# Queries turned raw in float32 and split behind the turn; tokens routed in four batches of blocks

## The chip, the cores and the metric

The kernel runs on one core of one Trainium2 chip. The metric is the device time of one execution in microseconds; of the kernel before, three runs gave 1262.17, 1265.66 and 1268.53 us, median 1265.66. One execution was profiled; it took 1265.35 us.

The engines are TensorE (PE in the profile, its weight loads PEld), VectorE (DVE), ScalarE (ACT), GpSimd (POOL) and SyncE (SP, which here only issues loads and stores). Each works off its own list of instructions in a fixed order.

## The reference, cut to what matters

Three layers follow each other: attention over the 32 largest scores of each query, a gated feed-forward layer on the normalized result, and a layer of 8 experts of which each token uses one.

```python
scores = scale * np.matmul(q, k.transpose(0, 1, 3, 2))        # 4 batches, 8 heads, 576 queries, 64 wide
kth = np.partition(scores, -32, axis=-1)[..., -32:-31]
scores = np.where(scores >= kth, scores, -1000000000.0)
attn = np.exp(scores - max); attn = attn / (attn.sum + 1e-9)
x = (attn @ v)                                                 # to 2304 tokens x 512
xn = x / sqrt(mean(x * x) + 1e-6) * rms_g
x = (silu(xn @ w_gate) * (xn @ w_val)) @ w_out                 # 512 -> 1536 -> 512
logits = x @ gate2 + modality_bias[modality_id]                # 8 experts
e_idx = argmax(logits); gate_w = softmax(logits)[e_idx]
out[mask_e] = gate_w * (relu(x[mask_e] @ w1[e]) @ w2[e])       # 512 -> 1024 -> 512
```

## The kernel before, in words

The kernel has a front, which computes attention, the feed-forward layer and the routing of the tokens, and a second part, which goes over the 8 experts.

**Attention.** The queries are cut into tiles of 128, and a step has two tiles; there are 72 steps (`steps`). For each tile TensorE makes the scores (`qk`, L526), ScalarE copies them to SBUF (L539), VectorE finds the 32nd largest score by rounds of MAX8 and MATCH_REPLACE8 (`topk`, L561 and L564, fed by L541 to L543), ScalarE and GpSimd mask and exponentiate (`soft0` to `soft3`), TensorE turns the result (`tr`, L621) and multiplies it by the values (`av`, L667). The scores need more precision than one pass of TensorE has, so every query is held as two float32r numbers: its rounded part and the rest.

**How a query is split before.** `dma_q` loads the two tiles of a step, 64 columns each. `split_q` makes the two parts on GpSimd: L452 rounds by adding zero, with each query written twice side by side, so that it lies in both halves of the 128 partitions after the turn; L453 subtracts the rounded part from the query. `trans_q` turns the four blocks (two tiles, two parts) on TensorE (L461), and one copy of 512 columns on ScalarE takes them out of PSUM into `qS` (L469, or L474 for the leftover queries). The load stands six steps ahead of the use, the split four, the turn two.

**Feed-forward layer.** As soon as all heads of a block of 128 tokens are done, the block, or a pair of blocks, is a granule; there are 17 granules with 18 blocks. A granule is a list of small pieces (`norm`, `xtr`, `ff1`, `ff2`), which `step` takes from a queue between the pieces of attention. The matrix products are in pairs of float16 parts, three products each (`mm3`, L746). The weights come in float32; VectorE picks their bits apart (`convert_weights`, L275, L280, L284), ScalarE makes the rounded part (L290, L292), GpSimd the rest (L293); the 12 pieces of `w_out` come first, the 24 of the other two later, while attention runs already. `gate_columns` folds the routing matrix into `w_out`, so `ff2` gives 8 more columns, the logits.

**Routing before.** Behind each granule, `ff2` adds the bias (L805) and calls `route`: 12 small VectorE instructions (L838 to L854) and one exponential on ScalarE find the expert, the one-hot `O` and the gate weight of each token of the granule. `rank`, a piece that goes into the queue of the next granule behind its first two products, counts on TensorE how many earlier tokens went to the same expert: for each block one product of a full matrix of ones with the sum so far `acc_oh` (L865), one of a triangle of ones with the block's own `O` (L866), and for the second block of a pair one with the first's `O` (L864). Its result stands in a bank of `ps_f`, of which there are two, shared with `ff1` and `ff2`. VectorE then adds (L875, L878, L879), makes slots (L880), advances `acc_oh` (L882), fills the payload (L884, L885), and GpSimd writes token number and weight into the expert's table by an indirect DMA per block (L887).

**What sets the order.** The program is written in the order of `step`, with high priority nowhere. The framework's scheduler then reorders each engine's list by a model of the times, so an edit at one place can move instructions far from it.

## Time and profile before

| | |
|---|---|
| runs | 1262.17, 1265.66, 1268.53 us |
| profiled execution | 1265.35 us, of which the span of instructions is 1263.7 us |
| busy, of the span | PE 90%, PEld 83%, DVE 73%, ACT 66%, POOL 58% |
| attention | ends near 828 us |
| feed-forward layer | first product at 171 us, last near 927 us |
| experts | from 946 us to the end |
| granted clock of TensorE | 0.929 of full speed over the span |

A busy time counts an engine as busy from the start of an instruction to its end. On TensorE and VectorE one instruction starts before the one ahead of it has ended, so busy times overlap; what an instruction costs its engine in a dense stretch is read from the start of one to the start of the next. In the tables of waits a line names the engine, tile and line that waited, then the engine, tile and line that released it, then the total in us, how many times, and the longest. The granted clock is given as a share of 2.4 GHz; 0.50 is the lower of its two levels, 1.2 GHz, and a value between is a mean over the stretch. In a row of the timeline "x4" means four instructions in a row, and the second number is from the start of the first to the end of the last.

### The profile page before, as it was taken

To read this page: it belongs to the slowest core of one execution; us is meant where nothing else is said; L and a number is where in the kernel's file an instruction comes from. 1 tells how busy PE (TensorE), PEld (TensorE's weight loads), DVE (VectorE), ACT (ScalarE), POOL (GpSimd) and SP (SyncE) were. 2 spreads that over 40 slices of the span, in tenths; PEclk is the share of its full clock that TensorE was granted. 3 is DMA by queue.
4 is the path that set the end of the run, shared out by engine and by line. 5 is a ranking of instruction groups with operands and counts; after the bars stand their busy time and mean duration, and the time that the engine had idled before them with its cause. 6 is when DMAs were issued, how large, how long until landed. Compare 5 with 4: busy or idle time off the path is not lost. (4 is left out here: it accounts for less than half of the span.)

```text
span 1263.7 us, 32277 instructions
## 1 busy us (share of the span) xinstructions
PE 1140.6 (90%) x12286; PEld 1044.3 (83%) x12286; DVE 927.7 (73%) x2883; ACT 833.3 (66%) x1757; POOL 738.8 (58%) x850
## 2 busy tenths in 40 slices
PE   6976777989999999999999999999948898999985
PEld 6965667988999999999898999999937897798884
DVE  7999999669999999999999999921115434254251
ACT  5868888677888888888998788753315434354251
POOL 7866767668857888777798767643423222022120
PEclk9856677989999999999999999999978998999998
DMA  8143312011000111000011000000029525354130
GB/s 289 51 126 84 96 44 79 14 45 48 9 17 17 28 40 53 17 8 18 23 38 40 17 15 10 2 11 19 2 71 348 185 73 209 109 184 139 70 116 18
DMA packets 68894, 87.80 MB, mean 69 GB/s; under 512 B 34386, under 2 KB 43734, under 8 KB 68696
## 3 DMA queue, kind: packets, MB, share of 16 engines
q1 hardware_dynamic: 60152, 63.66, 16.3%
q0 software_dynamic: 6320, 16.31, 3.8%
q10 hardware_dynamic: 2224, 5.25, 1.2%
q8 instruction: 117, 1.92, 0.7%
q14 instruction: 81, 0.66, 0.2%
HBM read 75.58 MB, written 10.92 MB: 68 GB/s over the span
## 5 line engine op out<-in xcount | busy, mean ns | idle before, releaser
L561 DVE MAX8 w<-w 128x8 f32<-128x296 f32 x576 | 249.8, 456 | 1.2
L595 POOL TENSOR_TENSOR s<-s,r 128x576 f32<-128x576 f32 x144 | 201.2, 1419 | 31.8 <-ACT r L591 31.5
L564 DVE MATCH_REPLACE8 w<-w 128x296 f32<-128x296 f32 x432 | 193.1, 449 | 0.0
L746 PE MATMUL pf<-xT,wg 128*128 128x128 f16 (+1 forms) x2448 | 172.5, 224 | 5.0 <-DVE T L875 2.9
L746 PE MATMUL pf<-xT,wv 128*128 128x128 f16 (+1 forms) x2448 | 168.8, 223 | 0.3 <-ACT xf L735 0.3
L746 PEld LDWEIGHTS <-wg 128*128 128x128 f16 x2448 | 148.8, 99 | 11.4 <-issue 5.4
L746 PE MATMUL po<-wo,h 128*128 128x264 f16 (+1 forms) x1296 | 157.4, 275 | 0.9 <-ACT t L773 0.9
L526 PE MATMUL ps<-kS,qS 128*128 128x288 f32 x640 | 138.4, 345 | 21.2 <-DVE w L542 20.3
L746 PEld LDWEIGHTS <-wv 128*128 128x128 f16 x2448 | 146.5, 98 | 4.6 <-issue 0.4
L746 PEld LDWEIGHTS <-h 128*128 128x128 f16 x1296 | 121.9, 98 | 18.8 <-issue 1.4
L1236 POOL DMA_INDIRECT out_dram<-o,idx x23 | 22.8, 993 | 195.7 <-ACT o L1235 139.6
L1180 DVE SCALAR_TENSOR_TENSOR hl<-ph,hh 128x256 fp32r<-128x256 f32 x88 | 36.9, 421 | 132.0 <-ACT hh L1179 129.0
L526 PEld LDWEIGHTS ps<-kS,qS 128*128 128x128 f32 x640 | 103.9, 215 | 24.4 <-ACT r L591 14.8
L599 ACT ACTIVATE s<-s,mbs 128x576 f32<-128x576 f32 x144 | 113.3, 788 | 13.5 <-POOL s L595 13.1
L1177 PE MATMUL ph<-xh,wh 128*128 128x256 f32 x352 | 101.5, 291 | 16.4 <-PEq L1294 16.0
L591 ACT ACTIVATE r<-s,mbs 128x576 f32<-128x576 f32 x144 | 104.9, 779 | 13.9 <-POOL mbs L582 13.8
L621 PE MATMUL pt<-identr,s 128*128 128x128 f32 x576 | 98.2, 302 | 14.8 <-ACT s L599 13.7
L539 ACT COPY s<-ps 128x576 f32<-128x576 f32 x144 | 93.2, 647 | 21.8 <-PE ps L526 21.2
L1177 PE MATMUL ph<-xl,wh 128*128 128x256 f32 x352 | 100.3, 286 | 0.0
L1177 PE MATMUL ph<-xh,wl 128*128 128x256 f32 x352 | 100.3, 286 | 0.0
L778 POOL TENSOR_TENSOR t<-u,t 128x512 f32<-128x512 f32 x54 | 69.6, 1290 | 48.1 <-ACT t L773 28.8
L667 PE MATMUL pt<-vs,pT 128*128 128x64 f16 (+1 forms) x1680 | 88.4, 198 | 8.7 <-POOL pT L635 6.0
(204 smaller groups left out, 2825.1 us busy)
## 6 DMA issues: line engine op xcount, KB each, us to landing
wr<-in_moe_w_dram SPq DMA_DIRECT2D x48, 512.0 KB
wst<-in_moe_w_gate_dram SPq DMA_DIRECT2D x24, 256.0 KB
wst<-in_moe_w_val_dram SPq DMA_DIRECT2D x24, 256.0 KB
wr<-in_moe_w_dram ACTq DMA_DIRECT2D x10, 512.0 KB
kr<-in_k_dram SPq DMA_DIRECT2D x32, 128.0 KB
vt<-in_v_dram SPq DMA_DIRECT2D x32, 128.0 KB
x_d<-xo SPq DMA_DIRECT2D x16, 256.0 KB
qr<-in_q_dram SPq DMA_DIRECT2D x112, 32.0 KB
```

Of the source, the lines that this page charges most:

```text
L526: nc.tensor.matmul(out=ps[:, a, 0:HS], lhsT=qS[i // 2][:, i % 2, j, o2:o2 + 128], rhs=kt[:, m, ks], start=(n == 0), stop=(n == len(ops) - 1),)
L539: nc.scalar.copy(out=s.rearrange("p (a k) -> p a k", a=2), in_=ps[:, :, 0:HS])
L561: steps.append(lambda: dve.max(lists[t][:, 8 * r:8 * r + 8], src[t] if r == 0 else dst[t]))
L564: steps.append(lambda: dve.match_replace(out=dst[t], in_to_replace=lists[t][:, 8 * r:8 * r + 8], in_values=src[t] if r == 0 else dst[t], i ...
L591: nc.scalar.activation(out=d["r"], in_=d["s"], func=AF.Relu, scale=-BIG, bias=d["mb"][:, 1:2])
L595: nc.gpsimd.tensor_tensor(out=d["s"], in0=d["s"], in1=d.pop("r"), op=OP.subtract)
L599: nc.scalar.activation(out=d["s"], in_=d["s"], func=AF.Exp, scale=SCALE, bias=d["mb"][:, 0:1], accum_out=d["rs"])
L621: nc.tensor.transpose(pt[:, c * 128:(c + 1) * 128], e[:, e0 + c * 128:e0 + (c + 1) * 128], ident)
L667: nc.tensor.matmul(out=av_[o:o + n], lhsT=l, rhs=r, start=(a == 0), stop=(a == len(ops) - 1))
L746: nc.tensor.matmul(out=out_, lhsT=l, rhs=r, start=(a == 0), stop=(a == len(ops) - 1))
L778: nc.gpsimd.tensor_tensor(out=t, in0=u, in1=t, op=OP.mult)
L1177: nc.tensor.matmul(out=pt, lhsT=l[:, fs], rhs=r[:, kk, :], start=(n == 0), stop=(n == 3 * KD - 1))
```

## The change

**Queries.** `dma_q` loads each query twice, into both halves of a tile of 128 columns, and does so four steps ahead instead of six. `split_q` is gone. `trans_q` turns the raw float32 queries, two blocks instead of four. Behind that ScalarE copies the 256 columns out of PSUM twice, once rounded to float32r straight into `qS` and once as they are into `qf`, and GpSimd subtracts one from the other into the second part of `qS`.

**Routing.** The granules are put into four batches that end with the granules 5, 10, 15 and 16: 6, 6, 5 and 1 blocks. `ff2` writes its logits into the batch's tile, and `route` and `rank` run once for a batch, behind its last granule, over all its blocks. In `rank` a block has one product with each earlier block of its batch. An assertion on the number of steps goes; nothing else changes.

```diff
+    NG = len(granules)
+    ENDS = [NG // 3, 2 * NG // 3 - 1, NG - 2, NG - 1]
+    batches = [
+        [blk for g in range(lo + 1, hi + 1) for blk in granules[g][1]] for lo, hi in zip([-1] + ENDS[:-1], ENDS)
+    ]
+    NBM = max(len(bl) for bl in batches)
...
         def dma_q(s):
-            qr = ap_.tile([128, 2, D], F32, name="qr", tag="qr", bufs=QB)
+            qr = ap_.tile([128, 2, 2, D], F32, name="qr", tag="qr", bufs=QB)
...
+            for j in range(2):
+                if hh is not None and t1[2] == hh:
+                    src = q[b, 2 * p + hh, 0:SM, :].rearrange("(p c) d -> p c d", c=CM)
+                    nc.sync.dma_start(out=qr[:, :, j, :], in_=src[:, c:c + 2, :])
+                    continue
...
-        def split_q(s):
-            qr = raw.pop(("q", s))
-            qs = ap_.tile([128, 2, 2, 2, D], F32R, name="qs", tag="qs", bufs=2)
-            z = zero.unsqueeze(2).unsqueeze(3).to_broadcast([128, 2, 2, D])
-            q2 = qr.unsqueeze(2).to_broadcast([128, 2, 2, D])
-            nc.gpsimd.tensor_tensor(out=qs[:, :, 0], in0=q2, in1=z, op=OP.add)
-            nc.gpsimd.tensor_tensor(out=qs[:, :, 1], in0=q2, in1=qs[:, :, 0].bitcast(F32), op=OP.subtract)
-            raw["qs", s] = qs
...
         def trans_q(s):
-            qs = raw.pop(("qs", s))
-            pt = ps_m.tile([128, 512], F32R, name="pq", tag="sm")
+            qr = raw.pop(("q", s))
+            pt = ps_m.tile([128, 512], F32, name="pq", tag="sm")
             for t in range(2):
-                for j in range(2):
-                    nc.tensor.transpose(
-                        pt[:, (2 * t + j) * 128:(2 * t + j + 1) * 128],
-                        qs[:, t, j].rearrange("p a d -> p (a d)"),
-                        identr,
-                    )
+                nc.tensor.transpose(
+                    pt[:, t * 128:(t + 1) * 128], qr[:, t].rearrange("p a d -> p (a d)"), ident
+                )
...
+            def post():
+                qf = ap_.tile([128, 2, 128], F32, name="qf", tag="qf", bufs=2)
+                nc.scalar.copy(out=hi, in_=cut(src))
+                nc.scalar.copy(out=qf, in_=src)
+                nc.gpsimd.tensor_tensor(out=lo, in0=cut(qf), in1=hi.bitcast(F32), op=OP.subtract)
...
-                at(s - 6, lambda s=s: dma_q(s))
+                at(s - 4, lambda s=s: dma_q(s))
...
-            at(s - 4, lambda s=s: split_q(s))
...
-                        if j == 0:
-                            rt["L"] = mp.tile([128, 2, E], F32, name="L", tag="L", bufs=1)[:, 0:nb]
+                        if bi not in logits:
+                            logits[bi] = mp.tile([128, NBM, E], F32, name="L", tag="L", bufs=1)
...
-                        if j == nb - 1:
+                        if j == nb - 1 and gi in ENDS:
                             route()
...
-                    for j in range(nb):
+                    for j in range(nr):
                         o = pt[:, j * E:(j + 1) * E]
                         for j2 in range(j):
                             nc.tensor.matmul(out=o, lhsT=ones16, rhs=O[:, j2, :], start=(j2 == 0), stop=False)
...
-            return pre, hid, res, [rank()]
+            return pre, hid, res, [rank()] if gi in ENDS else []
```

The instructions of `route` and of the second half of `rank` stay as they are, over `nr` blocks of the batch instead of `nb` of the granule.

The scheduler also orders the first tens of microseconds anew. On SP the loads of the program's start stand like this before (`qr` is the query tile, `kr` the keys; `wg`, `wv` with L262 are the pieces of `w_out`, which are loaded into the room of the other weights):

```order
L262 DMA wg_105<-in_moe_w_out_dram 128x1024 x2
L371 DMA kr<-in_k_dram 128x256
L374 DMA kr<-in_k_dram 64x64
L371 DMA kr<-in_k_dram 128x256
L374 DMA kr<-in_k_dram 64x64
L441 DMA qr<-in_q_dram 128x64 x2
L262 DMA wg_105<-in_moe_w_out_dram 128x1024
```

and after the change, from the load that follows the first keys on:

```order
L268 DMA wg_105<-in_moe_w_out_dram 128x1024
L268 DMA wg_106<-in_moe_w_out_dram 128x1024 x3
L151 DMA gate_sb<-in_moe_w_gate_dram 128x4x8
L152 DMA g_sb<-in_moe_rms_g_dram 128x4x1
L268 DMA wv_107<-in_moe_w_out_dram 128x1024 x3
L268 DMA wv_108<-in_moe_w_out_dram 128x1024
L377 DMA kr<-in_k_dram 128x256
L380 DMA kr<-in_k_dram 64x64
L377 DMA kr<-in_k_dram 128x256
L380 DMA kr<-in_k_dram 64x64
L268 DMA wv_108<-in_moe_w_out_dram 128x1024 x2
L450 DMA qr<-in_q_dram 128x64 x12
```

The first queries were the seventh load; now 22 loads stand ahead of them, all 12 pieces of `w_out` among these.

On GpSimd the first split of a query stood second in the work on the start's data (`ks` are the split keys, `wo` the rests of `w_out`, `qs` the split queries):

```order
L405 TENSOR_TENSOR ks<-kr,zero 128x9x64
L452 TENSOR_TENSOR qs<-qr,zero 128x2x128
L406 TENSOR_TENSOR ks<-kr,ks 128x9x64
L293 TENSOR_TENSOR wo_110<-wf,wo_109 128x2x256
L453 TENSOR_TENSOR qs<-qr,qs 128x2x128
```

and now the first difference that makes a query complete (L479) stands behind nine of the twelve rests:

```order
L412 TENSOR_TENSOR ks<-kr,ks 128x9x64
L299 TENSOR_TENSOR wo_110<-wf,wo_109 128x2x256 x3
L153 TENSOR_SCALAR gs_sb<-g_sb 128x4
L299 TENSOR_TENSOR wo_110<-wf,wo_109 128x2x256 x3
L411 TENSOR_TENSOR ks<-kr,zero 128x9x64
L299 TENSOR_TENSOR wo_110<-wf,wo_109 128x2x256
L412 TENSOR_TENSOR ks<-kr,ks 128x9x64
L208 MEMSET room 128x288
L299 TENSOR_TENSOR wo_110<-wf,wo_109 128x2x256
L209 IOTA room 128x144
L299 TENSOR_TENSOR wo_110<-wf,wo_109 128x2x256
L479 TENSOR_TENSOR qS<-qf,qS 128x2x128
```

On VectorE the first scores (`w<-s,ps`, then MAX) came behind 20 of the 36 instructions that pick apart `w_out` (`wp`):

```order
L275 TENSOR_SCALAR wp<-wv_107 128x512
L284 SCALAR_TENSOR_TENSOR wp<-wg_106,wp 128x512
L280 SCALAR_TENSOR_TENSOR wp<-wv_107,wp 128x512
L541 TENSOR_TENSOR w<-s,ps 128x288
L542 TENSOR_TENSOR w<-s,ps 128x288
L284 SCALAR_TENSOR_TENSOR wp<-wv_107,wp 128x512
L543 MAX w<-w 128x8
```

and now come behind all 36:

```order
L281 TENSOR_SCALAR wp<-wv_108 128x512
L286 SCALAR_TENSOR_TENSOR wp<-wv_108,wp 128x512
L290 SCALAR_TENSOR_TENSOR wp<-wv_108,wp 128x512
L547 TENSOR_TENSOR w<-s,ps 128x288
L548 TENSOR_TENSOR w<-s,ps 128x288
L549 MAX w<-w 128x8
```

From there on the two sorts of work, which were mixed, follow each other.

## Rows read from the trace of the kernel before

**Rows 1.** Windows; columns: stretch, length, busy (count) of PE, PEld, DVE, ACT, POOL; PEclk

```profile
60.00:220.00 160.00, 116.08 (x776) 101.75 (x775) 160.00 (x534) 130.26 (x277) 113.78 (x132) 0.66 0.30 86
220.00:340.00 120.00, 114.04 (x1483) 104.57 (x1483) 96.42 (x324) 92.29 (x205) 87.66 (x103) 0.95 0.11 30
340.00:820.00 480.00, 476.60 (x6392) 440.82 (x6392) 465.16 (x1581) 400.03 (x894) 367.43 (x425) 1.00 0.08 23
820.00:928.00 108.00, 105.85 (x1572) 100.37 (x1569) 25.37 (x132) 40.60 (x87) 44.45 (x46) 1.00 0.04 12
928.00:1263.00 335.00, 281.87 (x1771) 252.00 (x1770) 130.17 (x191) 128.35 (x211) 77.25 (x77) 0.92 0.42 143
```

**Rows 2.** Waits of PE between 340 and 820 us, the longest

```profile
PE pf L746 <- DVE u L768: 1.2, 1, 1.2
```

**Rows 3.** Timeline of PE at 507 us

```profile
507.27 0.94 PE L746 MATMUL pf<-xT,wv 128*128 128x128 f16 x14
508.05 0.61 PE L621 MATMUL pt<-identr,s 128*128 128x128 f32 x4
508.49 0.27 PE L626 MATMUL sm<-identr,s 128*128 128x128 f32 x1
508.52 0.54 PE L461 MATMUL pq<-identr,qs 128*128 128x128 f32 x4
508.90 1.18 PE L746 MATMUL pf<-xT,wv 128*128 128x128 f16 x18
```

**Rows 4.** Timeline of DVE at 525 us

```profile
525.19 0.14 DVE L838 TENSOR_REDUCE mx<-L 128x1 f32<-128x8 f32 x1
525.25 0.15 DVE L843 TENSOR_TENSOR d<-L 128x8 f32<-128x8 f32 x1
525.32 0.46 DVE L561 MAX8 w<-w 128x8 f32<-128x296 f32 x1
```

**Rows 5.** Line L878 on DVE: duration in ns, least, median, most

```profile
L878 DVE TENSOR_TENSOR T<-T,O x17: 154/346/1335, 276.0 to 926.6; 128x8 f32<-128x8 f32 x16, 128x16 f32<-128x16 f32 x1
```

**Rows 6.** Line L875 on DVE: who waited for it, us and times

```profile
  PE pf L746: 2.9, 6
  PE ps L526: 0.8, 1
```

**Rows 7.** Timeline of PE at a rank, 857 us

```profile
857.07 0.17 PE L866 MATMUL pr<-O,tri 128*128 128x8 f16 x1
857.57 2.84 PE L746 MATMUL pf<-xT,wg 128*128 128x128 f16 x48 [0.33 <-DVE T L875]
```

**Rows 8.** Turns of queries: L461 at 220 to 340 us, its group at 340 to 820 us

```profile
L461 PE MATMUL pq<-identr,qs x40: 225/249/366, 220.5 to 335.9; 128*128 128x128 f32 x40
...
L461 PE MATMUL pq<-identr,qs 128*128 128x128 f32 x172 | 24.0, 255 | 0.0
```

**Rows 9.** Timeline of SP and DVE in the first 20 us

```profile
17.78 4.10 SPq L441 DMA_DIRECT2D qr<-in_q_dram  x6
...
18.93 0.69 DVE L280 SCALAR_TENSOR_TENSOR wp<-wv,wp 128x512 int32<-128x512 int32 x1
19.53 0.45 DVE L541 TENSOR_TENSOR w<-s,ps 128x288 f32<-128x288 f32 x1
```

**Rows 10.** Waits of DVE between 0 and 60 us, the longest

```profile
DVE wp L275 <- DMA wg<-in_moe_w_out_dram: 4.3, 2, 2.6
```

**Rows 11.** Groups on POOL, 340 to 820 us: count, busy, mean ns, idle before

```profile
L595 POOL TENSOR_TENSOR s<-s,r 128x576 f32<-128x576 f32 x92 | 128.7, 1421 | 20.7 <-ACT r L591 20.4
...
L453 POOL TENSOR_TENSOR qs<-qr,qs 128x256 fp32r<-128x256 f32 x41 | 30.1, 734 | 1.4
...
L452 POOL TENSOR_TENSOR qs<-qr,zero 128x256 fp32r<-128x256 f32 x41 | 25.5, 621 | 22.0 <-PE pq L461 21.8
```

**Rows 12.** Timeline of POOL in the last granule

```profile
906.45 1.01 POOL L887 DMA_INDIRECT tab_d<-pay,si  x1 [0.15 <-issue]
910.90 1.28 POOL L778 TENSOR_TENSOR t<-u,t 128x512 f32<-128x512 f32 x1 [2.25 <-ACT t L773]
```

More of the change, by code (lines that the diff above doesn't have):

```diff
@@ L131, in topk_attention_swiglu_moe_kernel @@
     margin = const.tile([128, 1], F32, name="margin")
-    finite = const.tile([128, len(granules)], F32, name="finite")
+    finite = const.tile([128, len(batches)], F32, name="finite")
     sumsq = const.tile([128, 4], F32, name="sumsq")
@@ L472, in trans_q @@
[L472 to L474 removed]
+                hi, lo, cut = dst[:, :, 0], dst[:, :, 1], lambda x: x
+            else:
+                dst = qS[s] = ap_.tile([128, 2, 2, 192], F32R, name="qS", tag="qS", bufs=2)
+                nc.gpsimd.memset(dst[:, :, :, 64:128].bitcast(F32), 0.0)
+                heads = dst.rearrange("p t j (i r) -> p t j i r", i=3)
+                hi, lo = heads[:, :, 0, 0::2], heads[:, :, 1, 0::2]
+                cut = lambda x: x.rearrange("p t (i r) -> p t i r", i=2)
@@ L689, in granule @@
             G = 512 // n
+            bi, batch = next((i, bl) for i, bl in enumerate(batches) if blocks[0] in bl)
             x = [xn.pop(j) for j in blocks]
@@ L880, in post @@
                     last_ = nc.vector.tensor_copy(si, sl)
-                    for j in range(nb):
+                    for j in range(nr):
                         nc.vector.tensor_tensor(out=acc_oh, in0=acc_oh, in1=O[:, j, :], op=OP.add)
                     with tc.issue_after(last_.ins):
-                        nc.vector.tensor_copy(pay[:, :, 0], tok[:, blocks[0]:blocks[0] + nb])
+                        j = 0
+                        while j < nr:
+                            n2 = 1
+                            while j + n2 < nr and batch[j + n2] == batch[j] + n2:
+                                n2 += 1
+                            nc.vector.tensor_copy(pay[:, j:j + n2, 0], tok[:, batch[j]:batch[j] + n2])
+                            j += n2
                         nc.vector.tensor_copy(pay[:, :, 1].bitcast(F32), rt["gt"])
-                    for j in range(nb):
+                    for j in range(nr):
                         nc.gpsimd.indirect_dma_start(
```

56 lines of the change are left out of this document (25 added, 31 removed).

## The prediction

> **What bounds the kernel now.** I read the busy times by stage first [rows 1]. Five stretches show five different states. From 60 to 220 us DVE is busy for all of 160 us, while PE stands idle for 44 of them at a granted clock of 0.66: scores and the picking apart of weights share VectorE, and it sets the pace. From 340 to 820 us PE is busy for 476.6 of 480 us at full clock and DVE for 465.2, so both look full and the table alone doesn't decide. From 820 to 928 us PE works off what is left of the feed-forward layer, DVE being nearly idle. From 928 us on the experts run, which the change doesn't touch: 335 us on both sides.
>
> Which of the two bounds the long stretch is read from the waits and from start-to-start times. PE's longest wait of the whole 480 us is 1.2 us [rows 2]. Busy times of PE overlap, so I check in the timeline that it is really dense [rows 3]: 14 float16 products of 128 columns take 0.78 us from the first start to the next group, 56 ns each, where 128 columns at 2.4 GHz need 53; the groups follow without a gap. PE is full there in earnest. DVE is less full than it looks: a routing instruction is counted with 0.14 us, but the next one starts 0.06 to 0.07 us later [rows 4]. So from 220 to 928 us I count every piece of work by what it takes from PE, and before 220 us by what it takes from DVE.
>
> **Turning the queries.** Four float32r turns of a step hold PE for 508.90 - 508.52 = 0.38 us; four float32 turns of another tile take 508.49 - 508.05 = 0.44 us, so the two new ones take 0.22 [rows 3]. A step saves 0.16 us. Of the turns 40 lie between 220 and 340 us and 172 between 340 and 820 us [rows 8]; at four a step these are 10 + 43 = 53 steps: **-8.5 us**. The other 19 steps lie in the stretch that DVE sets, and I count them at nothing; the cover there is DVE's own 160 us. The end of this term towards more: two float32 turns at the float32r pace, 0.19 us a step, -10.
>
> A float32 operand could be dearer than that. The row says that a float32 turn costs 0.11 us against 0.095 for float32r [rows 3]. By the Trainium skill, page "FP8 and Floating Point Precision", section "TensorE Precision Notes", a true float32 operand goes through the array in four passes, and one pass rounds it; that speaks against turning raw queries. The trace does not agree for turns: 0.11 us is not four times 0.056.
>
> **Waits at the ranks.** A rank's result holds one of the two banks that the next products need, and PE waits until DVE has read it: 2.9 + 0.8 = 3.7 us in seven recorded waits [rows 6]. A part is hidden in overlapping busy times: at 857 us the next product starts 0.50 us behind the last of the rank, of which 0.33 are recorded [rows 7]. At 0.50 for each of 17 ranks it would be 8.5 us. Four ranks stay, so 13 of 17 parts go: -2.8 by the recorded waits, -6.5 by that row. I take **-4**, nearer to the record, since ten ranks show no wait at all. Against it stand more products in a rank: with batches of 6, 6, 5 and 1 blocks there are 15 + 15 + 10 = 40 products with earlier blocks where there was one. They have 8 columns; none should hold PE longer than one of 128 columns, 0.056 us, so 39 of them cost at most **+2** and at least nothing.
>
> **VectorE.** A routing has some 19 small instructions at 0.07 us [rows 4] and one of 0.35 in the median [rows 5], 1.6 us; 13 fewer give back 21 us of DVE, spread over 250 to 928 us. I count this at nothing, because PE is full without it. What it does is to leave PE as the only bound.
>
> **ScalarE and GpSimd.** ScalarE gets one copy more in a step, with half the columns in each. Even a whole microsecond for it would be 43 us of the 80 that ACT is idle from 340 to 820 [rows 1]: nothing. GpSimd loses the rounding, 0.62 us, and keeps one subtraction of 0.73 [rows 11]; it is no bound. But this subtraction now stands between the turn and the scores, see the third rival.
>
> **SP and the start.** Loads of queries double, 152 more over some 800 us. In the steady part SP waits for free tiles, so I count them at nothing. At the start it is different: SP issued 26 loads until 17.78 us [rows 9], 0.65 us each, so 22 loads ahead of the first query put its issue near 15 us, where it was the seventh. Behind the load stand the turn, two copies and the nine rests on GpSimd that the order shows. VectorE's first scores came at 19.53 us behind 20 instructions on `w_out`; 16 more of these at 0.60 us [rows 9] bring them to about 29 us. They are work that has to be done anyway, and DVE is full until 220 us, so a swap of the two costs **0** as long as DVE finds something to do. The cover ends near 29 us: then `w_out` is used up and only the scores are left. If DVE stands for as long as the scores come later, that is +9. In the other direction, DVE now waits 4.3 us for `w_out` [rows 10], whose loads move ahead: -3.
>
> **220 to 340 us.** PE is idle for 6 of 120 us at a clock of 0.95 [rows 1]: attention has run dry and fills again. Two ranks stand there; these are counted. The rest would give at most 6 - 2 of idle time and 6 for the clock, -10, if the new order fills it, and 0 if not. I take **-2**, nearer to 0, because nothing in the change is made for that place.
>
> **The end.** The batch of five ends with the last granule but one, so GpSimd issues five indirect writes of 1.01 us where it issued one at 906.45 us; the next job comes at 910.90 behind an idle time of 2.25 us [rows 12]. Four more fit almost; their jobs run between products that PE still has. I count 0, and +2 without this cover.
>
> **Sum.** -8.5 - 4 + 2 + 0 - 2 = -12.5 us against the profiled execution of 1265.35 us (span 1263.7 and 1.65 around it), which stands 0.3 us below the median of the runs: **1253 us**, 1.0% less. With all terms at their good ends: -10 - 6.5 - 3 - 10, some -29; with all at the bad ones: -8.5 - 2.8 + 2 + 9 + 2, +2.
>
> **Rivals.** A measurement of this kernel tells about 0.5%, 6.3 us, from no change.
>
> *First, more than that (below 1246 us).* The stretch from 220 to 340 us fills up, or DVE did hold PE up in the long stretch by more than the recorded waits: 21 us off DVE then add to the 8.5 of the turns, 1236. For it: DVE's 97% [rows 1]. Against: PE's spacing. 0.15.
>
> *Second, the start eats it (1259 to 1272).* DVE runs out of work behind `w_out`, while the turn, the copies and GpSimd fill the attention anew: +9 there makes it 1262. For it: everything for the first scores now comes through one more engine. Against: the picking apart that it is swapped with is the same work. 0.23.
>
> *Third, slower.* The scores of a step wait on GpSimd. A query is complete only when the subtraction has run, and it queues behind masks of 1.42 us [rows 11]. If PE stood for 0.37 us at each of 53 steps, this would eat the 12.5 us and 6.3 more; at half a microsecond it would be 26.5 - 12.5 = +14, near 1279, and at the full 1.42 us of a mask near 1328. Against: the turn stands a whole step ahead of the use, and GpSimd is idle 113 of 480 us [rows 1]. From 1272 on: 0.10.
>
> *Fourth, four passes.* If a raw float32 turn does cost four products of 0.056 us, two take 0.45 us against 0.38 now: +0.07 in 53 steps, +3.7 for -8.5, 1265. The trace has 0.11 us for the same instruction [rows 3]; 0.02. This is the rule of the Trainium skill's page named above.
>
> That the change doesn't do what it says can be left out: the instructions show two turns a step and four ranks.
>
> **How the numbers follow.** The forecast, 1246 to 1259, gets 0.50. Faster by over 0.5% is the forecast and the first rival, 0.65; within 0.5% the second and the fourth, 0.25; slower the third, 0.10. The range leaves out the far part of the first rival below 1240 and the third with the worst of the start above 1267: **1240 to 1267 us**.
>
> **What would show it.** Right: in the stretch of mixed work, PE still without waits, the group of query turns with half the instructions at 0.11 us from start to start, PE waiting for the rank's reading in a few places only; DVE with more idle time at an unchanged PE share; first scores near 29 us and the end of the DVE stretch near 220. Wrong: idle time of PE ahead of L532 released by GpSimd's L479 (third rival); idle time of DVE between 30 and 60 us (second); DVE's share in the long stretch unchanged at a shorter stretch (first).

## The result, and the profile after

The changed kernel takes 1282.1 us in the median (1279.8 to 1286.4), the kernel before 1267.1 us in the same comparison: ratio 1.0121, 95% interval 1.0098 to 1.0144. It is slower by 15 us, where 12.5 us less were forecast. The profiled execution took 1283.25 us, its span is 1281.4 us against 1263.7 us.

Windows of the changed kernel by stage, with the columns of [rows 1]:

```profile
60.00:220.00 160.00, 114.63 (x733) 99.16 (x732) 158.68 (x530) 129.47 (x288) 104.53 (x118) 0.63 0.33 92
220.00:340.00 120.00, 113.46 (x1447) 103.07 (x1445) 84.14 (x263) 88.52 (x203) 80.29 (x86) 0.94 0.13 33
340.00:820.00 480.00, 467.83 (x6158) 428.65 (x6156) 437.36 (x1368) 387.64 (x898) 330.00 (x374) 0.99 0.11 29
820.00:928.00 108.00, 106.92 (x1589) 101.00 (x1587) 50.46 (x164) 58.83 (x125) 53.52 (x57) 1.00 0.03 9
928.00:1263.00 335.00, 296.77 (x1971) 265.44 (x1969) 133.85 (x214) 131.63 (x219) 82.95 (x85) 0.93 0.42 142
```

From 340 to 820 us PE stands idle for 12 us where it stood 3.4, at a clock of 0.99 instead of 1.00, and VectorE has 28 us less to do. So neither is as full as it was. In the last row lie 19 us of the feed-forward layer, which before was done by 928 us.

Where the 17.7 us of span came in is read from the timeline at four marks. The last picking apart of weights starts at 231.07 us (before 226.85): +4.2. From there to the logits of the last granule but one it takes 687.3 us (673.7): +13.6. From these to the last logits 29.0 us (22.2): +6.8. So the last logits start 24.6 us later, at 947.3 us against 922.7. From the last logits to the first transposition of the experts it is 23.7 us in both. The experts, whose code is the same, take 7.0 us less (310.3 against 317.2); 5.3 of these are PE's waits for its own sequencer behind the experts' branches (16.0 us before, 10.7 after), the rest was not followed.

Windows of 20 us of the changed kernel, those in which PE loses most:

```profile
500.00:520.00 20.00, 14.36 (x220) 13.13 (x217) 17.89 (x49) 11.68 (x27) 12.99 (x13) 0.99 0.18 27
520.00:540.00 20.00, 20.00 (x227) 17.96 (x227) 18.61 (x61) 13.97 (x33) 17.66 (x22) 0.92 0.21 53
740.00:760.00 20.00, 18.54 (x296) 17.55 (x294) 19.90 (x72) 14.09 (x34) 9.39 (x11) 1.00 0.11 29
760.00:780.00 20.00, 16.86 (x215) 15.41 (x212) 16.30 (x53) 12.43 (x28) 13.85 (x16) 0.91 0.04 6
920.00:940.00 20.00, 16.36 (x264) 15.23 (x262) 4.94 (x19) 4.17 (x9) 9.16 (x9) 0.90 0.02 2
```

These are the three places at which a batch ends: behind the granules 5, 10 and 15. PE stands idle there, and the granted clock is lower within 20 us of it. The timeline of GpSimd at the first of them (start, length, count; in brackets the idle time before and what ended it):

```profile
502.46 1.25 POOL L902 DMA_INDIRECT tab_d<-pay,si  x1 [0.55 <-DVE pay L900]
503.79 0.19 POOL L611 TENSOR_SCALAR sums<-sums 128x2 f32<-128x2 f32 x1
506.59 1.00 POOL L902 DMA_INDIRECT tab_d<-pay,si  x1 [2.61 <-DMA tab_d<-pay,si]
507.59 1.32 POOL L785 TENSOR_TENSOR t<-u,t 128x512 f32<-128x512 f32 x1
508.83 0.23 POOL L588 TENSOR_TENSOR mbs<-w,cst 128x6 f32<-128x6 f32 x1
512.09 1.02 POOL L902 DMA_INDIRECT tab_d<-pay,si  x1 [3.04 <-DMA tab_d<-pay,si]
513.14 1.16 POOL L641 TENSOR_TENSOR pT<-pf,pT 128x512 f16<-128x512 f32 x1
514.26 1.16 POOL L787 TENSOR_TENSOR h<-t,h 128x512 f16<-128x512 f32 x1
```

and PE in the same microseconds:

```profile
514.36 0.47 PE L673 MATMUL pt<-vs,pT 128*128 128x64 f16 x10 [2.96 <-POOL pT L641]
...
518.63 0.63 PE L532 MATMUL ps<-kS,qS 128*128 128x288 f32 x3 [1.66 <-DVE w L548]
```

A table write (L902, before L887) doesn't start until the one before it has landed. The likely reason, which no run tests, is that the places in `tab_d` are known only at run time, so that the program must take each write to touch what the last one wrote. GpSimd works in order, so while the third write waits from 509 to 512 us, the weights `pT` of the attention (L641) and `h` of the feed-forward layer (L787) wait behind it, and PE behind these: 2.96 us. The second wait of PE, 1.66 us, is not shown to come from the writes: VectorE had stood for 2.11 us behind ScalarE's L396, which waited for a load, and its next instruction, L397, took 3.17 us (0.49 in the median). The writes of the kernel before (L887) stood alone, a granule apart, but for one pair, and had landed when the next one came.

At the second batch the way to PE is longer. VectorE, GpSimd and ScalarE, one fence for each engine:

```profile
760.44 0.46 DVE L567 MAX8 w<-w 128x8 f32<-128x296 f32 x1
...
770.11 0.46 DVE L547 TENSOR_TENSOR w<-s,ps 128x288 f32<-128x288 f32 x1 [3.37 <-ACT s L545]
```

```profile
765.62 0.97 POOL L902 DMA_INDIRECT tab_d<-pay,si  x1 [2.89 <-DMA tab_d<-pay,si]
...
767.29 0.20 POOL L588 TENSOR_TENSOR mbs<-w,cst 128x6 f32<-128x6 f32 x1
```

```profile
767.53 1.44 ACT L597 ACTIVATE r<-s,mbs 128x576 f32<-128x576 f32 x2 [3.89 <-POOL mbs L588]
```

The small instruction L588 makes `mbs` from the largest and the 32nd largest scores of a step. They were ready when VectorE's MAX8 of 760.44 us had ended (the eighth of that step; each step has eight), but L588 stood behind the second and the third write until 767.29. ScalarE waited for `mbs`, its copy of the next scores (L545) stood behind that, VectorE waited for the copy, and PE for VectorE, 2.73 us until 771.08. So a wait that the tables put down to VectorE can go back to GpSimd.

The view of DMA issues gives the time from issue to landing, 4.3 us in the median:

```profile
tab_d<-pay,si POOLq DMA_INDIRECT x18, 4.3
```

and the view of GpSimd's groups from 340 to 820 us says what 12 such writes cost its list (count; busy, mean ns; idle before, and what ended it): 12.7 us of waiting for each other, for 12.4 us of work.

```profile
L902 POOL DMA_INDIRECT tab_d<-pay,si x12 | 12.4, 1032 | 14.9 <-DMA tab_d<-pay,si 12.7 <-DVE pay L900 1.6 <-issue 0.3
```

The Trainium skill, page "DMA: Bandwidth & Descriptors", section "Anatomy of one DMA — SWDGE (gpsimd) path", says that a wait on a semaphore happens on the sequencer that issues the DMA, and gives some 2.0 us of fixed time for one. The trace agrees with the first: the 3.04 us ahead of the third write above stand in GpSimd's own list. For the second it has 4.3 us from issue to landing in these writes of 128 rows of 8 bytes; the measurement decides.

In the last granule it is plainest. GpSimd, VectorE and PE of the changed kernel, one fence for each engine:

```profile
925.38 1.07 POOL L902 DMA_INDIRECT tab_d<-pay,si  x1 [1.26 <-DVE pay L900]
926.49 1.17 POOL L787 TENSOR_TENSOR h<-t,h 128x512 f16<-128x512 f32 x1
929.87 0.99 POOL L902 DMA_INDIRECT tab_d<-pay,si  x1 [2.21 <-DMA tab_d<-pay,si]
932.83 0.97 POOL L902 DMA_INDIRECT tab_d<-pay,si  x1 [1.97 <-DMA tab_d<-pay,si]
933.82 1.28 POOL L785 TENSOR_TENSOR t<-u,t 128x512 f32<-128x512 f32 x1
```

```profile
936.34 0.69 DVE L775 SCALAR_TENSOR_TENSOR u<-u,pf 128x512 f32<-128x512 f32 x1 [9.19 <-ACT u L774]
```

```profile
937.08 4.34 PE L753 MATMUL po<-wo,h 128*128 128x264 f16 x19 [3.37 <-DVE u L775]
```

The product `t` of 933.82 us stands behind the third write; ScalarE's cast of it, the next tanh on ScalarE, and `u` on VectorE follow one after the other, and the last products start late.

### The profile page after: what moved, and what is told of

Its sections match the earlier page's. It is cut to its first block, busy times and chain, and to the rows that moved or that the text cites. A ratio compares the mean times of both kernels' runs of the same rounds, so it can differ in the third digit from the quotient of the medians.

```text
span 1281.4 us, 32130 instructions
## 1 busy us (share of the span) xinstructions
PE 1146.6 (89%) x12181; PEld 1041.2 (81%) x12181; DVE 913.0 (71%) x2652; ACT 836.4 (65%) x1816; POOL 692.9 (54%) x778
## 5 line engine op out<-in xcount | busy, mean ns | idle before, releaser
L601 POOL TENSOR_TENSOR s<-s,r 128x576 f32<-128x576 f32 x144 | 201.0, 1416 | 37.6 <-ACT r L597 37.3
L532 PE MATMUL ps<-kS,qS 128*128 128x288 f32 x640 | 142.4, 349 | 35.6 <-DVE w L548 27.0
L753 PE MATMUL pf<-xT,wg 128*128 128x128 f16 (+1 forms) x2448 | 172.4, 224 | 1.3 <-DVE T L884 0.7
L753 PE MATMUL pf<-xT,wv 128*128 128x128 f16 (+1 forms) x2448 | 169.9, 224 | 2.4 <-ACT wf L298 2.2
L753 PE MATMUL po<-wo,h 128*128 128x256 f16 (+1 forms) x1296 | 164.2, 281 | 5.7 <-DVE u L775 3.4
L753 PEld LDWEIGHTS <-wv 128*128 128x128 f16 x2448 | 148.7, 99 | 7.6 <-issue 1.9
L753 PEld LDWEIGHTS <-wg 128*128 128x128 f16 x2448 | 148.4, 99 | 7.1 <-issue 1.0
L753 PEld LDWEIGHTS <-h 128*128 128x128 f16 x1296 | 126.4, 100 | 27.6 <-issue 6.5
L545 ACT COPY s<-ps 128x576 f32<-128x576 f32 x144 | 93.3, 648 | 32.1 <-PE ps L532 31.2
L1193 PE MATMUL ph<-xh,wh 128*128 128x256 f32 x352 | 101.3, 291 | 13.6 <-PEq L1310 10.7
L673 PE MATMUL pt<-vs,pT 128*128 128x64 f16 (+1 forms) x1680 | 93.6, 198 | 13.7 <-POOL pT L641 9.1
L1145 DVE TENSOR_TENSOR wl<-wr,wh 128x1024 fp32r<-128x1024 f32 x64 | 76.4, 1221 | 24.7 <-ACT wh L1144 24.2
```

Source lines behind the costliest of these rows:

```text
L532: nc.tensor.matmul(out=ps[:, a, 0:HS], lhsT=qS[i // 2][:, i % 2, j, o2:o2 + 128], rhs=kt[:, m, ks], start=(n == 0), stop=(n == len(ops) - 1),)
L545: nc.scalar.copy(out=s.rearrange("p (a k) -> p a k", a=2), in_=ps[:, :, 0:HS])
L601: nc.gpsimd.tensor_tensor(out=d["s"], in0=d["s"], in1=d.pop("r"), op=OP.subtract)
L673: nc.tensor.matmul(out=av_[o:o + n], lhsT=l, rhs=r, start=(a == 0), stop=(a == len(ops) - 1))
L753: nc.tensor.matmul(out=out_, lhsT=l, rhs=r, start=(a == 0), stop=(a == len(ops) - 1))
L1145: nc.vector.tensor_tensor(out=lo, in0=w[0], in1=hi.bitcast(F32), op=OP.subtract)
```

## The experiments

The theory from the traces is **W**: the writes of a batch wait for each other and hold up GpSimd's list. Its rivals: **S**, the late first queries cost at the start; **D**, VectorE is level with PE, so that what the queries gain depends on VectorE's load; **O**, the scheduler's new order alone is worth some us in either direction. Each ratio is against the kernel before in the same comparison, with its 95% interval.

### The two halves

The query part of the change alone, with the routing of before:

```diff
-            at(s - 4, lambda s=s: split_q(s))
...
+                at(s - 4, lambda s=s: dma_q(s))
...
             return pre, hid, res, [rank()]
```

> Only the queries are changed (loaded twice, turned raw, split behind the turn); the routing is that of the kernel before, behind each granule. Theory W (the table writes of a batch wait for each other and hold up GpSimd, and that eats the gain of the turns): no batch is left, so the turns give their 8 to 10 us and the start takes some 4 back: about 1261 us, ratio 0.995 (0.990 to 0.999). Theory S (the late first queries and the subtraction on GpSimd ahead of the scores are what costs): at least as slow as the change itself, 1272 to 1282 us, with idle time of PE ahead of the scores. Theory O (any new order of the scheduler costs or gives some 10 us by chance, over the clock): anywhere between 1255 and 1285, and the sum of the two halves does not make the whole.

Measured: 1277.2 us, ratio 1.0085 (1.0059 to 1.0111). W alone fails: no batch, and yet 10 us slower. The time is one that S allows, and PE does stand ahead of the scores, but not for the subtraction on GpSimd that S named. The longest waits of PE between 340 and 820 us, by that kernel's lines (engine and line that waited, what for; us, times, longest):

```profile
PE ps L524 <- DVE w L540: 4.2, 6, 1.6
PE pt L665 <- DVE pT L635: 3.9, 6, 1.1
```

PE waits for VectorE, 8.1 us in twelve places, where the kernel before had 1.2 us in one as its longest [rows 2]. This is what made me form D. The end of the stretch that VectorE sets came at 235.0 us, 8 us late.

The routing part alone, with the queries of before (`split_q`, four turns, loads six steps ahead):

```diff
+            return pre, hid, res, [rank()] if gi in ENDS else []
...
             at(s - 4, lambda s=s: split_q(s))
```

> Only the routing is changed (four batches); the queries are split on GpSimd ahead of the turn as before. Theory W: the whole loss without the gain: 15 plus some 6, about 1288 us, ratio 1.016 (1.010 to 1.022), with GpSimd waiting in three places for writes to tab_d. Theory S: 1260 to 1267, the ranks' waits gone. Theory O: anything in between.

Measured: 1275.1 us, ratio 1.0066 (1.0043 to 1.0089). Slower as W said, though by 8 us and not by 21, below W's range. PE waits for `pT` on GpSimd for 3.25 us at 504.14 us and 2.57 us at 761.54 us in it; both times `pT` stands on GpSimd right behind or one short instruction behind a write that had waited for the one before it, for 3.32 and 4.35 us. From the last logits but one to the last it takes 27.4 us.

### The writes

One write for each batch. This kernel leaves out the writes of the other 14 blocks, so their tokens don't come into the tables; the experts do the same amount of work on an empty row for them:

```diff
-                    for j in range(nr):
+                    for j in range(1):
                         nc.gpsimd.indirect_dma_start(
```

> The change with the table write of the first block of each batch alone: the tokens of the other 14 blocks do not come into the tables, and the experts work on the empty row for them at the same counts, so that all other work stays. Theory W: GpSimd does not wait any more, PE gets back 5.6 us of idle time at 500 to 520, 4.6 at 740 to 780, 6.6 in the last granule and the clock lost behind them: 1282 - 18, about 1264 us (1258 to 1270). Theory S: 1278 to 1284, as the change. Theory O: could be either.

Measured: 1253.6 us, ratio 0.9890 (0.9831 to 0.9948): 28 us less than the change, 10 more than I gave to W and outside W's range.

The same five stretches in it, one 20 us earlier at the end because the kernel is that far ahead (windows, columns of [rows 1]):

```profile
500.00:520.00 20.00, 19.76 (x236) 18.02 (x234) 18.52 (x61) 14.05 (x31) 15.73 (x18) 0.93 0.14 37
520.00:540.00 20.00, 20.00 (x285) 18.91 (x285) 18.75 (x61) 17.27 (x42) 12.67 (x17) 1.00 0.13 29
740.00:760.00 20.00, 19.97 (x315) 18.00 (x312) 20.00 (x62) 13.85 (x30) 10.93 (x13) 1.00 0.07 16
760.00:780.00 20.00, 20.00 (x215) 18.13 (x215) 17.24 (x57) 14.74 (x35) 12.89 (x15) 0.91 0.04 9
...
900.00:920.00 20.00, 19.74 (x315) 19.01 (x313) 5.42 (x23) 5.56 (x10) 8.55 (x8) 1.00 0.01 3
```

PE is busy for 99.5 of the 100 us where it was for 86.1.

All writes kept, those of the first two batches set apart:

```diff
-                            nc.gpsimd.tensor_tensor(out=h[:, 1], in0=t, in1=h[:, 0], op=OP.subtract)
+                            r = nc.gpsimd.tensor_tensor(out=h[:, 1], in0=t, in1=h[:, 0], op=OP.subtract)
+                            if writes:
+                                with tc.issue_after(r.ins):
+                                    writes.pop(0)()
...
+                    now_ = 1 if bi < 2 and not exact else nr
+                    for j in range(now_):
+                        write(j)
+                    writes.extend(lambda j=j: write(j) for j in range(now_, nr))
```

> The change with the writes of the first two batches apart: one at the rank and one more behind each later rest of h on GpSimd, at least 5 us apart; the batch of five in the tail is left as it is. Theory W: two of three stalls go, 10 us of idle time and some clock: 1282 - 11, about 1271 us (1266 to 1276), and the tail still has its 29 us from the last logits but one to the last. Theory S: 1278 to 1284. Theory O: could be either.

Measured: 1260.2 us, ratio 0.9954 (0.9929 to 0.9979), 22 us less than the change, twice what I gave to W here. From the last logits but one to the last it still takes 28.7 us.

And the granules of the tail routed singly, so that no batch of five is left there:

```diff
-    ENDS = [NG // 3, 2 * NG // 3 - 1, NG - 2, NG - 1]
+    ENDS = [NG // 3, 2 * NG // 3 - 1, *range(2 * NG // 3, NG)]
```

> The spread writes of the first two batches, and the last granules routed one by one, so that no batch of five stands in the tail. Theory W: the third stall goes too; from the last logits but one to the last it takes 22.5 us and not 28.7: 1260 - 6, 1254 us (1250 to 1258), that is where the kernel with one write per batch came out, which has the same products and no stall. Rival (GpSimd had room in the tail, and the 6 us there are an accident of the order): 1260 as with two spread batches.

Measured: 1255.1 us, ratio 0.9920 (0.9891 to 0.9949). This is the best version: it leaves nothing out, routes in 8 batches instead of 4, and is 11 us under the kernel before and 27 under the change, as W said. From the last logits but one to the last it is 22.2 us, against 28.7 with the batch of five. Its first writes on GpSimd, 10 us and more apart, wait for nothing of weight:

```profile
490.35 1.25 POOL L905 DMA_INDIRECT tab_d<-pay,si  x1 [0.99 <-PE pt L673]
500.64 1.01 POOL L905 DMA_INDIRECT tab_d<-pay,si  x1 [0.15 <-issue]
513.83 1.02 POOL L905 DMA_INDIRECT tab_d<-pay,si  x1 [0.16 <-issue]
```

### VectorE's load

The routing with two spread batches, but with the old queries:

> The old way of the queries (split on GpSimd ahead of the turn, four float32r turns) with the routing in batches and the writes of the first two spread; against the same with the new queries (1260 us) this tells what the queries alone are worth once the stalls are gone. If PE is the bound and the turns give 10 us of it, less 4 at the start: 1260 + 6, 1266 us. If the queries are worth nothing (VectorE bounds beside PE, the start takes it back): 1256 to 1261. If the queries cost 10 us, as they seemed to with the routing of before: 1250.

```diff
-                at(s - 4, lambda s=s: dma_q(s))
+                at(s - 6, lambda s=s: dma_q(s))
...
+            at(s - 4, lambda s=s: split_q(s))
```

Measured: 1268.4 us, ratio 1.0021 (1.0001 to 1.0040). So the new queries are worth 8.1 us less time beside the spread batches, and 10.5 us more beside the routing by granule. Neither half gains alone in this order; both differences are no larger than what the order alone moves (below).

VectorE's work of a routing put back behind the 13 granules that end no batch, into tiles that nobody reads:

```diff
-                        if j == nb - 1 and gi in ENDS:
-                            route()
+                        if j == nb - 1:
+                            route() if gi in ENDS else spare()
...
-            return pre, hid, res, [rank()] if gi in ENDS else []
+            return pre, hid, res, [rank() if gi in ENDS else spare_rank()]
```

> The kernel with two spread batches (1260 us), and behind each of the 13 granules that end no batch the VectorE work of a routing again, 19 small instructions and an exponential on tiles that nobody reads; no product on PE, no bank of PSUM. Theory D (with the turns made cheaper PE and VectorE are level, and VectorE's 21 us of routings are what the queries' gain needs): back toward the kernel with new queries and routing by granule, 1260 + 10 to 17: 1270 to 1277. Theory P (the ranks cost PE through their bank, VectorE has room): 1260 to 1262. Theory O (the order by chance): no rule.

Measured: 1273.3 us, ratio 1.0063 (1.0037 to 1.0090): 13 us more than with two spread batches, as D said, 1.0 us for each spare routing. PE's longest wait from 340 to 820 us is again one for VectorE:

```profile
PE ps L532 <- DVE w L548: 5.1, 4, 1.8
```

Ahead of three of these four VectorE had no idle time, so it was VectorE's own work that PE waited for; ahead of the fourth, 1.7 us, VectorE had itself stood for 3.4 us behind L588 on GpSimd.

The same with two products for each block in a bank of PSUM that VectorE reads:

```diff
+                        pt = ps_f.tile([128, 512], F32, name="pr", tag="f")
...
+                            nc.tensor.matmul(out=o, lhsT=ones16, rhs=sp["O"][:, j, :], start=True, stop=False)
+                            nc.tensor.matmul(out=o, lhsT=tri, rhs=sp["O"][:, j, :], start=False, stop=True)
```

> As the run before, and each of the 13 spare routings with its two products per block in a bank of PSUM that VectorE reads. Theory D: like the run before, within 3 us. Theory P: 4 us and more above the run before, 1264 to 1268 where that stands at 1260; from the forecast's term 13 x 0.3 = 4.

Measured: 1270.8 us, ratio 1.0048 (1.0023 to 1.0074). The products and their bank cost nothing that can be told on top of the work of VectorE.

### The start

The loads of the first three steps' queries two steps earlier, in the change and in the best version:

```diff
-                at(s - 4, lambda s=s: dma_q(s))
+                at(s - (6 if s < 3 else 4), lambda s=s: dma_q(s))
```

> The change with the loads of the first three steps' queries two steps earlier, so that the first query is the seventh load again; the rest as in the change. Theory W+S (three stalls at the batches are most of the loss, and some 4 us come from the start: there VectorE waits 5.0 us for the first scores where it waited 1.3): the first scores come near 20 us, weights are picked apart near 227 us, the stalls stay: 1282 - 4, 1278 us (1274 to 1282). Theory W alone: 1282 and the end of the VectorE stretch where it was, near 231. Theory S alone: under 1270.

Measured: 1282.7 us, ratio 1.0146 (1.0100 to 1.0193). The first scores do come at 16.95 us, but VectorE then stands for 5.7 us (its waits in the first 60 us), because GpSimd is late with the first sums:

```profile
DVE sums L616 <- POOL sums L611: 5.7, 1, 5.7
```

GpSimd's timeline has the reason: it stood for a load of the modalities, and the mask of the first tiles (`s`, L601) came behind that and the rounding of the next keys (L411).

```profile
39.97 0.20 POOL L187 CAST room<-room 128x18 f32<-128x18 int32 x1 [5.05 <-DMA room<-in_moe_modality_id_dram]
...
43.34 1.15 POOL L411 TENSOR_TENSOR ks<-kr,zero 128x576 fp32r<-128x576 f32 x1 [0.23 <-DMA kr<-in_k_dram]
44.44 1.41 POOL L601 TENSOR_TENSOR s<-s,r 128x576 f32<-128x576 f32 x1
```

The stretch that VectorE sets ends at 239.9 us, 9 us later than in the change.

> As the run with spread writes and single routings in the tail, and with the early loads of the first three steps' queries. Theory W+S: 4 us less than that run, 1250 us (1246 to 1255). Theory W alone: the same as that run, 1254. Theory O (each new order is worth plus or minus some us by chance): more than that run is as likely as less.

Measured, in the best version: 1269.2 us, ratio 1.0033 (1.0009 to 1.0057), 14 us more than without the early loads, where 4 less or nothing was expected.

The first three steps in the old way (`split_q`, four turns), the rest new, in the best version and in the one with new queries alone:

```diff
+            if s < QO:
+                at(s - 3, lambda s=s: split_q(s))
+            at(s - 2, lambda s=s: (trans_q0 if s < QO else trans_q)(s))
```

> The best so far (spread writes, single routings in the tail, 1255 us) with the first three steps' queries split and turned in the old way and loaded once, six steps ahead, and the new way from the fourth step on. The stretch that VectorE sets ended at 226.9 us in both kernels with old queries and the old start that were looked at last, at 229 to 235 with the new ones. If that start costs: it ends near 227 again and the whole takes 1255 - 4, 1251 us (1247 to 1254). If not: 1255 to 1258.

> New queries from the fourth step on, the first three in the old way, and the routing of the kernel before, behind each granule. With all queries new this took 1277 us. If the start is what costs there (its VectorE stretch ended 8 us late): 1269 us. If VectorE and PE in the long stretch cost it (10 us of PE's waits on VectorE): 1273 to 1277. If the turns alone counted: 1258.

Measured: 1270.1 us, ratio 1.0018 (0.9996 to 1.0041), and 1274.8 us, ratio 1.0064 (1.0042 to 1.0087). In the first the stretch that VectorE sets ended at 227.9 us, as hoped, and 3.5 us were won there; then the long stretch took 20 us more, with PE busy for 472.5 of 480 us at a clock of 0.98. S falls as the main cause: what is won or lost at the start doesn't decide. (The kernel before in a third order, below, ends that stretch at 206.3 us, 20 us earlier, and takes 2 us less in all.) From the fourth step on these edits change the order alone.

### The order

One edit without any work of its own, which makes the scheduler order everything anew, on four kernels (the second order); and another on two (the third):

```diff
-        KT, KU = 3, 1
+        KT, KU = 3, 0
```

```diff
-                at(s - 2, lambda b=b, p=p: dma_v(b, p))
+                at(s - 3, lambda b=b, p=p: dma_v(b, p))
```

> The kernel before with one edit that changes no work: the turn of the leftover keys stands one step earlier in the program, and the scheduler then orders all engines anew (some 7,500 lines of PE's order differ). Theory W+D (stalls behind the batch writes; VectorE's relief): within 4 us of the kernel before, 1262 to 1270. Theory O (a new order is worth ten us either way by chance): 1255 to 1280, and the differences between the kernels do not survive a second order.

> The changed kernel with the same edit. Theory W+D: its three stalls stay in the new order, and it is 15 us (10 to 20) slower than the kernel before with that edit; near 1282. Theory O: the difference lies anywhere between -10 and +30.

> The kernel with spread writes and single routings in the tail with the same edit. Theory W+D: 11 us (6 to 16) faster than the kernel before with that edit, and 26 us (20 to 32) faster than the changed kernel with it; near 1255. Theory O: no such rule; as slow as 1270 would be no surprise.

> The run before, and behind each of the 9 granules that end no batch the VectorE work of a routing again, on tiles that nobody reads. In the first order 13 of these cost 13 us. Theory D (VectorE's relief carries the gain): 9 us (5 to 13) slower than the run before. Theory O: the same as that run, or faster.

> A third order for the kernel before: the loads of the values stand one step earlier in the program, no work changes (some 8,200 lines of PE's order differ). If the order given is a lucky one among others, it is slower than before, 1268 to 1280; if the second order was an unlucky one, 1262 to 1270.

> The same for the changed kernel. Sum by the mechanisms (the gain of the turns and of the ranks against the waits of the writes, of which the 5 to 6 us in the tail stood in both orders): between 5 us faster and 15 us slower than the kernel before in this order. Theory O: the sign of the difference changes with the order, and the mean over the three orders is within 8 us of nothing.

Medians in us, and in brackets the ratio to the kernel before as given, with its interval:

| order | before | changed | best version | best, VectorE's work put back |
|---|---|---|---|---|
| as given | 1267.1 | 1282.1 (1.0098 to 1.0144) | 1255.1 (0.9891 to 0.9949) | not run |
| second | 1275.9 (1.0040 to 1.0112) | 1271.7 (1.0025 to 1.0068) | 1266.3 (0.9984 to 1.0023) | 1273.6 (1.0034 to 1.0079) |
| third | 1263.0 (0.9968 to 1.0010) | 1282.2 (1.0085 to 1.0164) | not run | not run |

The order alone moves a kernel by up to 13 us, more than most terms of the forecast. The difference of the change is +15, -4 and +19 us in the three orders: its sign is not the same in all, its mean is +10. That is on O's side; by W and D the kernel before should have moved by 4 us at most. What survives the second order: the best version is 11 us under the kernel before in the first, 10 in the second; VectorE's work costs 13 us for 13 granules in the first, 7 for 9 in the second, 1.0 and 0.8 us each; and with a batch of five the last granule takes 4.8 to 6.8 us longer in all three orders (29.0, 27.0 and 28.7 us against 22.2 in each). The last is the firmest: in all nine kernels here that write five blocks there it takes 25.9 to 29.0 us, in the ten that route singly there 22.2, and 22.6 in the one that keeps the batch and writes one block. VectorE's price is less firm. That PE waits for its work is in the second order too, 5.2 us at 492.3 us with no idle time of VectorE ahead; but the two edits of the first three steps in the best version, without any such work, cost 14 and 15 us. What doesn't survive: the 27 us between the change and the best version are 5 in the second order. There the waits at `tab_d` on GpSimd, from 340 to 960 us, come to little more than half of what they were as given. Three fences, the change in the order given, the second and the third:

```profile
POOL tab_d L902 <- DMA tab_d<-pay,si: 19.3, 10, 3.0
```

```profile
POOL tab_d L902 <- DMA tab_d<-pay,si: 10.9, 8, 2.3
```

```profile
POOL tab_d L902 <- DMA tab_d<-pay,si: 9.6, 7, 2.2
```

In the third they are no longer than in the second, and the kernel is 11 us slower: how much a wait costs depends on what stands behind it. In that order PE is busy for 15.00 us of 20 at the second batch:

```profile
760.00:780.00 20.00, 15.00 (x151) 12.71 (x148) 14.45 (x48) 11.63 (x25) 14.01 (x16) 0.91 0.04 7
```

The start of the last logits, up to which nearly all that the change touches has run, tells more than the whole. Each figure is from one profiled execution, in the order given, the second and the third. The kernel before has them at 922.7, 930.8 and 924.1 us, the change at 947.3, 934.1 and 942.8: later by 24.6, 3.4 and 18.8 us, in every order. That the change is faster as a whole in the second order comes from behind this mark, 333.6 us against 343.5 for code that is nearly the same. The best version has them at 920.1 and 927.3 us, only 2.7 and 3.5 us earlier than the kernel before; the rest of its gain in these executions lies behind the mark, most of it in the experts. Why these take from 310 to 319 us in the kernels here, with the same code, was not followed.

Taken together, the four runs with the change's queries and all writes of a batch next to each other (the change in three orders, and with early loads) took 1271.7 to 1282.7 us, 1279.7 in the mean. The five with these queries whose first two batches at least have spread writes, and without spare work on VectorE, took 1255.1 to 1270.1, 1264.2 in the mean. The kernel before has 1268.7 in the mean of its three orders. By these means, an estimate over unlike orders, the writes cost some 15 us, and some 4 are left of the gain.

## Why the prediction was wrong

The step that failed is the pricing of GpSimd, "it is no bound" and "The end", 0 or +2: it took a table write for its issue. The next write waits until it has landed, and GpSimd's other work, and with it PE, waits behind it. By the prediction's own steps:

- **Turning the queries, -8.5: right in size, not banked.** Two float32 turns take 0.22 us from start to start, as counted. PE's timeline of the changed kernel:

```profile
381.92 0.38 PE L460 MATMUL pq<-identr,qr 128*128 128x128 f32 x2
382.14 1.06 PE L753 MATMUL po<-wo,h 128*128 128x264 f16 x8
```

  Summed from each start to the next, between the end of the VectorE stretch and the last logits, the turns hold PE for 11.7 us instead of 21.9. With spread batches the time falls by 8.1 us; with the routing by granule it rises by 10.5.
- **Waits at the ranks, -4 + 2: the record went as said, but it was no time.** PE's wait for the rank's reading is one of 0.7 us between 340 and 868 us (`PE pf L753 <- DVE T L884`), in place of [rows 6]. The products of 13 spare routings in that bank cost nothing beside VectorE's own work, in one order.
- **VectorE, 0: wrong, as far as the runs tell.** "I count this at nothing, because PE is full without it." The work put back costs 0.8 to 1.0 us of time for each granule, in two orders, by differences that the order alone can make. The amount was nearly right: the routing's lines, each from its start to the next but at most its own duration, take VectorE 43 us before and 20 after, 24 less where 21 were counted. That PE is dense in one sample of the timeline [rows 3] didn't show that VectorE never ended a wait in a kernel with less work for PE.
- **GpSimd, "it is no bound", and the end, 0 or +2: these failed.** Here the sign was lost. "Four more fit almost" took a write for 1.01 us of issue [rows 12]; the next one waits until it has landed, 4.3 us. The term was applied in one place of three: the batches at the granules 5 and 10 end in the middle of the long stretch, and got no price at all. At the end it measured 4.8 to 6.8 us; all three together, the change against the best version, 27 us in the order given and 5 in the second, the order's own share included.
- **SP and the start, 0 (-3 to +9): within its bounds.** First scores at 29.9 us (29 forecast), the VectorE stretch 4.2 us later. Its end "near 220" was no sign to go by: it lay at 226.9 us before already, and at 231.1 after. Putting the loads back didn't give the 4.2 us back.
- **220 to 340 us, -2: nothing came**; PE is busy for 113.46 us where it was for 114.04 [rows 1].
- **The rivals.** The second showed its sign in part: VectorE stands for 4.0 us at 42 us until scores come. The third had the sign of the result, by another mechanism: no wait of PE for the subtraction L479 stands in the record of the change. GpSimd's queue was the place, with the table writes ahead instead of the masks. The fourth is out: a turn of raw float32 took 0.11 us.

Whether the sum would have stood without the stalls is not shown. The best version has the same turns, and is 11.1 us under the kernel before in the order given and 9.6 in the second, where 12.5 were forecast; but all of the 12.5 lay ahead of the last logits, and there it gains 2.7 and 3.5 us. That its whole comes near the forecast is luck in part. The range had no term for the order, which is worth up to 13 us here.

Open: how the stalls and the order share the 15 us. The change is slower by 10 us in the mean of three orders; the tail's 4.8 to 6.8 us are in each of them, the other two stalls come and go with what stands behind the writes. Open too is what the order and the experts add by themselves.

## What to carry to other kernels

Indirect writes to one tensor, put next to each other on a queue that also computes, cost here the landing of each and not its issue; spread them behind the queue's other work, or keep them one at a time. Two engines that are both at 97% or more can share the bound: price what is taken off either of them as a pair, since here, in the order given, either half of the change lost time and both together (without the stalls) gained. Where a scheduler orders the program, make one more order by an edit without work, for both kernels, before a difference of 1% is put down to the change, and compare the kernels at a mark behind the last work that was changed.

## What the runs showed that was not expected

- Lone table writes and batched ones take the same time to land, 4.1 us in the median before and 4.3 after; what differs is only who stands behind them.
- PE's granted clock stands lower within 20 us of a stall of a few microseconds: 0.92 at 520 to 540 us behind 5.6 idle us, 0.91 at 760 to 780. That the stall lowers it is not shown. With one write for each batch it stood at 0.93 and 0.91 in two of the five windows above, with PE busy for 19.76 and 20.00 of the 20 us. In the change it also stood at 0.83 from 380 to 400 us, where PE was busy for all of the 20 us: at 1.2 GHz from 390.0 to 396.8, behind three microseconds in which PE had mostly run the attention's short products of 64 columns (L673), many of them one by one.
